# An attention block and two MLPs on one core: results of the second MLP turned by VectorE in 32 by 32 blocks and stored with short runs

## The chip, the cores and the metric

The kernel runs on one core of one Trainium2 chip. The metric is the device time of one execution in microseconds (us). The five engines are TensorE (PE, with its weight loads as PEld), VectorE (DVE), ScalarE (ACT), GpSimd (POOL) and SyncE (SP), which here issues nearly all transfers between the on-chip memory (SBUF) and the device's memory. The transfers of the core run on 16 transfer engines (DMA).

## What is computed

```python
# q, k, v: (8, 8, 576, 64) float32
q_s = softmax(q, axis=-1); k_s = softmax(k, axis=2)
x = q_s @ (k_s.T @ v)                       # per batch and head
x = x.transpose(0, 2, 1, 3).reshape(4608, 512)
h = x @ moe_w_in                            # (512, 2048)
x = (h * clip(h + 3, 0, 6) / 6) @ moe_w_out # (2048, 512)
h = x @ moe2_w_in
out = (h * sigmoid(h)) @ moe2_w_out         # (4608, 512) float32
```

The products are kept near float32 accuracy by splitting each operand into an upper and a lower part and adding three products (upper by upper, upper by lower, lower by upper).

## The kernel before

The 4608 rows are cut into nine blocks of 512. Attention and most of the first MLP run first (`first_block`, `middle`). From about 731 us on, `second_mlp` works in five passes (`PASSES`), each over two neighbouring blocks: four passes of the second MLP, on blocks 1 and 2, 3 and 4, 5 and 6, 7 and 8, and, after the first of them, one pass of the first MLP on blocks 7 and 8. Block 0 comes last, in a plain loop. The passes use seven products in place of eight (Strassen's scheme), on sums of quarters of the weights that were stored to memory (`ws`) before.

A pass has 56 inner steps (`inner`, L1330, products with the first weight matrix, tile `pb`) and 56 outer steps (`outer`, L1500, products with the second one), six matmuls of 128x512 each, one step after the other on TensorE. The weights come through a ring of six places (`ring`): a place holds two parts, each of which serves one step, and `fetch` (L1177, 512 KB) fills it again once its last step is done, for the step that comes six places later. Meanwhile `x_ahead` prepares the operands of the next pass: loads (L1460, tile `xst`), splits on ScalarE and VectorE (tile `gsp`), stores to `xd` (L1470, L1471) and later a load back.

The order is written out by hand: `when(t, fn)` files a piece of work under a time counted in steps, the list is sorted by this time, and every engine gets its instructions in that order. SP works through its list in order too: a transfer that waits for data holds up those behind it. Successive transfers of SP use eight completion counters (DMAHW0 to DMAHW7) in turn, and each waits until the one eight before it has landed.

At the end of a pass of the second MLP the result lies in eight tiles of 128x512 (`fixed`), transposed: rows are columns of the result, columns are the 512 rows of a block. `turn` brings it into place. It runs eight times per pass, every five steps from about four steps after the pass's end on, that is, between the inner steps of the next pass (`bank` gives it one of eight PSUM banks in turn). For the last pass of all, it runs in the loop over block 0, once in each of its first eight steps, with a bank of `a_pool`. One `turn` makes four transposes of 128x128 on TensorE against the identity `ident` (L1545, four matmuls with an identity operand), copies the 128x512 result from PSUM to SBUF on ScalarE (L1549, tile `o2`, which the trace and the order call `o`) and stores it with one transfer of 256 KB (L1551), in which each of the 128 partitions writes one run of 2 KB.

The operation that the change uses stands already in the stage before: `q_blocks` (L479) turns a 128x512 tile on VectorE in blocks of 32 by 32, `q_store` writes it, and `q_load` (L489) reads it back with four transfers of 32 partitions and runs of 128 B.

Of the kernel before, what the change touches and what calls it, by code (L numbers as in the profile page):

```python
# [18 lines left out]
P = 128  # L19
BLK = 512  # L20
# [8 lines left out]
def efficient_attention_then_two_mlps(  # L29
# [11 lines left out]
    nc = tc.nc  # L41
# [4 lines left out]
    NC = DM // P  # L46
    NF = DFF // P
    NB = NT // BLK
    NCH = BLK // P
# [6 lines left out]
    PASSES = ((1, 1), (0, NCL)) + tuple((1, j) for j in range(3, NB, 2))  # L56
# [14 lines left out]
    ident = const.tile([P, P], F32, name="ident")  # L71
# [4 lines left out]
    small = const.tile([P, 8], F32, name="small")  # L76
# [637 lines left out]
    for i, u in enumerate(range(2, NP)):  # L714
        o = i * (KB + VB + QB)
# [115 lines left out]
    for j in range(1, NB):  # L831
        for pr in range(NP):
            n = (j - 2) * NP + pr
# [326 lines left out]
    def when(t, fn):  # L1160
        ev.append((t, len(ev), fn))
# [7 lines left out]
    def bank():  # L1169
        pool, tag = BANKS[taken[0] % 8]  # L1170
        taken[0] += 1
        return pool.tile([P, 512], F32, tag=tag, name="pb")
# [126 lines left out]
    def second_mlp(last):  # L1299
        fixed = []  # L1300
# [12 lines left out]
        def small(name, tag="t2k"):  # L1313
            return tmp.tile([P, BLK], F32, tag=tag, bufs=1 if tag == "r" else 5, name=name)
# [4 lines left out]
        d = {}  # L1319
# [214 lines left out]
            for k, (name, m) in enumerate((name, m) for name in names for m in range(2)):  # L1534
                when(t + k, lambda m=m, name=name: do(m, name))

        def turn(j, k, bank=bank):

            h, i = (1, k) if k < NCH else (0, k - NCH)
            at = bank()  # L1540
            for a in range(2):
                for m in range(2):
                    x = fixed[4 * m + ((3, 1), (0, 2))[a][h]]
                    c = 2 * a + m
                    nc.tensor.transpose(  # L1545
                        at[:, c * P : (c + 1) * P], x[:, i * P : (i + 1) * P], ident
                    )
            o = small("o2")
            nc.scalar.copy(o, at)  # L1549
            rows = out[(j + h) * BLK : (j + h + 1) * BLK, :].rearrange("(p i) d -> i p d", i=NCH)  # L1550
            nc.sync.dma_start(rows[i], o)  # L1551

        T = 0.0
        uses = {}
        BB = len(PASSES)
        for b, (ph, j) in enumerate(PASSES):
# [35 lines left out]
            if b + 1 < BB:  # L1592
# [6 lines left out]
                            lambda n=n, low=low: x_fetch(n, low),  # L1599
                        )  # L1600
                for k in range(2 * NCH if ph else 0):
                    when(T + 3.95 + 5.0 * k, lambda j=j, k=k: turn(j, k))
            else:
                def begin_last():
                    op.pop("spare")
# [20 lines left out]
        for f in range(NF):  # L1626
            s = (1, 0, f)
            mm1(s)
            if f < 2 * NCH:
                turn(PASSES[-1][1], f, a_pool)  # L1630
            gate(s, lambda: None)
            if prev is not None:
                mm2(prev)
            if f % 2 == 0:
                load_split(f + 1, 1)
            prev = s
# [57 lines left out]
```

## Time and profile before

| | us |
|---|---|
| median of three runs | 1607.06 (1603.67 to 1607.39) |
| profiled execution | 1605.05 |
| its span, first to last instruction | 1603.3 |
| TensorE busy | 1573.6 |
| VectorE busy | 1130.5 |
| ScalarE busy | 790.1 |
| GpSimd busy | 447.6 |

The span is a little shorter than the time of the execution. A line of the profile names a group of instructions by its line in the kernel, its engine and its operation, and gives what it writes and reads (`out<-in`). Matmuls overlap, so that their durations cannot be added up; the distance between starts tells their cost. The share of the DMA engines is the mean over all 16.

The results are turned in four stretches: from 890 to 946 us (blocks 1 and 2), from 1199 to 1256 us (3 and 4), from 1354 to 1412 us (5 and 6), and from 1510 to 1552 us (7 and 8, in the loop over block 0). They are called the first to the fourth stretch below.

### The profile page before, as it was taken

The page shows a single profiled execution, that of the slowest core. Times are in us where ns is not written, and L with a number is a line of the kernel's source. Part 1 is how long each engine was busy: PE and PEld are TensorE (multiplying, and loading weights), DVE is VectorE, ACT ScalarE, POOL GpSimd, SP SyncE. Part 2 cuts the span into 40 slices and gives each one's busy share as a digit, 9 for nine tenths or more (in the row PEclk, how much of TensorE's full clock was granted, in tenths as well). Part 3 has the DMA queues.
Part 4 walks back from the last instruction along what each step waited for, and adds up shares of the span by engine and source line. Part 5 has one row for each costly group of instructions (what it writes and reads, how often), then busy time and mean ns, then how long its engine had stood idle before and what let it go on. Part 6 is the DMA issues. An engine that isn't in the chain of part 4 may idle for free.

```text
span 1603.3 us, 23117 instructions
## 1 busy us (share of the span) xinstructions
PE 1573.6 (98%) x7516; PEld 1288.0 (80%) x7516; DVE 1130.5 (71%) x1882; ACT 790.1 (49%) x1422; POOL 447.6 (28%) x417
## 2 busy tenths in 40 slices
PE   5999999999999999999999999999999999999998
PEld 3777888887878888888888888888888888888887
DVE  8989567777777787676877667667757775567522
ACT  5777345555554555454454445444534553445322
POOL 2002233334233344542410451045005500330000
PEclk9999999999999999999999999999999999999999
DMA  9913976777767776858987898898979886669730
GB/s 269 333 30 113 322 220 208 206 227 220 239 203 220 223 233 200 249 171 295 366 295 286 297 356 301 315 315 307 331 256 329 323 329 236 215 229 356 247 125 27
DMA packets 352426, 401.61 MB, mean 250 GB/s; under 512 B 120497, under 2 KB 233137, under 8 KB 352305
## 3 DMA queue, kind: packets, MB, share of 16 engines
q1 hardware_dynamic: 350256, 399.05, 74.6%
q8 instruction: 60, 0.98, 0.2%
q10 hardware_dynamic: 2048, 1.08, 0.2%
q14 instruction: 62, 0.50, 0.1%
HBM read 276.56 MB, written 123.47 MB: 250 GB/s over the span
## 4 chain that ended last, share of the span: by engine, by line
PE 93%; DMA 3%; SPq 2%; DVE 1%; ACT 1%; issue 0%; POOL 0%; ACTq 0%; DVEq 0%; POOLq 0%
PE pb L1500 24%; PE pb L1330 24%; PE h L562 20%; PE y L634 18%; PE y L636 3%; PE pa L516 2%; PE pa L398 1%; DMA wi_early<-in_moe_w_in_dram 1%; PE pb L1545 1%; DMA wo_early<-in_moe_w_out_dram 1%; SPq L100 0%; SPq L106 0%; DMA zd<-qz 0%; DMA ws<-fa 0%; DMA qraw<-in_q_dram 0%
## 5 line engine op out<-in xcount | busy, mean ns | idle before, releaser
L1330 PE MATMUL pb<-xo,ring 128*128 128x512 f32 x1680 | 390.6, 391 | 0.4 <-ACT s L1370 0.4
L562 PE MATMUL h<-x,wi 128*128 128x512 f32 x1536 | 381.5, 395 | 3.7 <-ACT g L610 1.9
L1500 PE MATMUL pb<-gsp,ring 128*128 128x512 f32 x1680 | 382.4, 389 | 0.0
L1500 PEld LDWEIGHTS pb<-gsp,ring 128*128 128x128 f32 x1680 | 315.3, 188 | 65.5
L1330 PEld LDWEIGHTS pb<-xo,ring 128*128 128x128 f32 x1680 | 313.3, 188 | 66.3 <-ACT s L1370 1.5
L562 PEld LDWEIGHTS h<-x,wi 128*128 128x128 f32 x1536 | 284.6, 189 | 67.1 <-ACT g L610 3.8
L634 PE MATMUL y<-g,wo 128*128 128x512 f32 x1344 | 326.3, 392 | 1.2 <-DVE o L653 1.2
L634 PEld LDWEIGHTS y<-g,wo 128*128 128x128 f32 x1344 | 252.4, 189 | 54.7 <-DVE o L653 1.6
L1317 DVE TENSOR_TENSOR gsp<-g,gsp 128x512 fp32r<-128x512 f32 x240 | 171.5, 722 | 72.1 <-ACT gsp L1435 69.2
L1435 ACT CAST gsp<-g 128x512 fp32r<-128x512 f32 x240 | 144.3, 622 | 139.4 <-DVE gsp L1317 70.1
L575 ACT ACTIVATE r<-h 128x512 f32<-128x512 f32 x112 | 66.9, 597 | 177.0 <-PE h L562 173.7
L1317 POOL TENSOR_TENSOR s<-U,s 128x512 f32<-128x512 f32 x32 | 44.7, 1395 | 383.7 <-DVE U L1317 368.7
L599 DVE SCALAR_TENSOR_TENSOR h<-r,h 128x512 f32<-128x512 f32 x112 | 77.5, 692 | 77.6 <-ACT r L575 77.1
L1317 DVE TENSOR_TENSOR g<-r,pb 128x512 f32<-128x512 f32 x96 | 65.6, 683 | 47.6 <-ACT r L1344 47.5
L1344 ACT ACTIVATE r<-pb 128x512 f32<-128x512 f32 x96 | 57.1, 595 | 70.9 <-DVE pb L1317 60.1
L437 POOL TENSOR_TENSOR qe<-qraw,qm 128x512 f32<-128x512 f32 x34 | 40.2, 1181 | 172.1 <-DVE qz L479 130.3
L590 ACT CAST g<-h 128x512 fp32r<-128x512 f32 x112 | 65.6, 585 | 45.5 <-DVE h L599 37.6
L1317 POOL TENSOR_TENSOR g<-g 128x512 f32<-128x512 f32 x40 | 54.9, 1372 | 91.9 <-DVE g L1317 79.9
L593 DVE TENSOR_TENSOR g<-h,g 128x512 fp32r<-128x512 f32 x96 | 66.0, 687 | 20.3 <-ACT g L590 18.9
L463 POOL TENSOR_TENSOR qe<-qe,qs 128x512 f32<-128x512 f32 x36 | 39.5, 1097 | 122.0 <-DVE qs L459 96.7
L195 POOL TENSOR_TENSOR fa<-fa 128x256 f32<-128x256 f32 x64 | 49.6, 775 | 55.3 <-DVE sp L227 50.2
L1317 DVE TENSOR_TENSOR U<-pb,s 128x512 f32<-128x512 f32 x80 | 54.7, 684 | 13.6 <-PE pb L1330 8.4
(166 smaller groups left out, 1830.4 us busy)
## 6 DMA issues: line engine op xcount, KB each, us to landing
ring<-ws SPq DMA_DIRECT2D x280, 512.0 KB, 5.1
ws<-sp SPq DMA_DIRECT2D x256, 128.0 KB, 2.2
xd<-gsp SPq DMA_DIRECT2D x112, 256.0 KB, 5.5
xo<-xd SPq DMA_DIRECT2D x56, 512.0 KB, 6.0
wi_early<-in_moe_w_in_dram SPq DMA_DIRECT2D x16, 512.0 KB, 9.0
wo_early<-in_moe_w_out_dram SPq DMA_DIRECT2D x16, 512.0 KB, 8.9
wi_raw<-in_moe_w_in_dram SPq DMA_DIRECT2D x16, 512.0 KB, 4.8
ws<-w_sum SPq DMA_DIRECT2D x64, 128.0 KB, 2.0
```

Of the source, the lines that this page charges most:

```text
L195: lambda to=to, x=x, y=y, op=op: nc.gpsimd.tensor_tensor(out=at[to], in0=at[x], in1=at[y], op=op)
L562: nc.tensor.matmul(h, w[:, a, c, :], x[:, e, c, :], start=(c == 0 and n == 0), stop=(c == NC - 1 and n == 2),)
L575: nc.scalar.activation(self.r, self.h, AF.Relu, bias=3.0)
L590: nc.scalar.copy(self.g[:, 0], self.r)
L593: nc.vector.tensor_tensor(out=self.g[:, 1], in0=self.r, in1=f32(self.g[:, 0]), op=ALU.subtract)
L599: nc.vector.scalar_tensor_tensor(out=self.h, in0=self.r, scalar=6.0, in1=self.h, op0=ALU.min, op1=ALU.mult)
L634: nc.tensor.matmul(y[c], w[:, a, cs], g[:, e, :], start=st, stop=sp)
L1317: (eng or nc.vector).tensor_tensor(out=out, in0=a, in1=b, op=how)
L1330: nc.tensor.matmul(to, ws_[:, a], e[:, c], start=p in ("P1", "P6", "P5") and c == 0 and m == 0, stop=c == 1 and m == 2, skip_group_check=True,
L1344: nc.scalar.activation(r, d[b, n, key], AF.Sigmoid)
L1435: nc.scalar.copy(t[0], source(p, i))
L1500: nc.tensor.matmul(d[b, p][m], w[:, a, m * P : (m + 1) * P], t[e], start=new and i == 0 and k == 0, stop=i == NPR - 1 and k == 2, skip_gro ...
```

## The change

`turn` gives way to `turn_blocks`, which is called at the same times, eight times per pass. Each call takes one of the eight result tiles (128 columns of the result by 512 rows), transposes it on VectorE in 64 blocks of 32 by 32, and stores it with four transfers of 32 partitions, 64 KB each; a partition then writes 16 runs of 32 numbers (128 B). The first call of a pass writes into a new tile `o2`, each later one into the tile whose contents were transposed by the call before (`gone`). TensorE, ScalarE and PSUM have no part in it any more.

```diff
-        def turn(j, k, bank=bank):
-
-            h, i = (1, k) if k < NCH else (0, k - NCH)
-            at = bank()
-            for a in range(2):
-                for m in range(2):
-                    x = fixed[4 * m + ((3, 1), (0, 2))[a][h]]
-                    c = 2 * a + m
-                    nc.tensor.transpose(
-                        at[:, c * P : (c + 1) * P], x[:, i * P : (i + 1) * P], ident
-                    )
-            o = small("o2")
-            nc.scalar.copy(o, at)
-            rows = out[(j + h) * BLK : (j + h + 1) * BLK, :].rearrange("(p i) d -> i p d", i=NCH)
-            nc.sync.dma_start(rows[i], o)
+        gone = []
+
+        def turn_blocks(j, k):
+            h, n = (1, k) if k < NC else (0, k - NC)
+            a, m = divmod(n, 2)
+            x = fixed[4 * m + ((3, 1), (0, 2))[a][h]]
+            o = gone.pop() if k else small("o2")
+            gone.append(x)
+            nc.vector.transpose(o, x)
+            rows = out[(j + h) * BLK : (j + h + 1) * BLK, n * P : (n + 1) * P]
+            for i in range(4):
+                e = slice(i * 32, i * 32 + 32)
+                nc.sync.dma_start(
+                    rows[:, e].rearrange("(b r i) c -> r i b c", b=4, i=NCH),
+                    o[e].rearrange("r (i b c) -> r i b c", i=NCH, b=4),
+                )
...
-                    when(T + 3.95 + 5.0 * k, lambda j=j, k=k: turn(j, k))
+                    when(T + 3.95 + 5.0 * k, lambda j=j, k=k: turn_blocks(j, k))
...
-                turn(PASSES[-1][1], f, a_pool)
+                turn_blocks(PASSES[-1][1], f)
```

SP at the start of the first stretch, before (`o` is the turned tile, `xst` and `xd` belong to the operands of the next pass; the brackets name what an instruction waits for):

```order
L1460 DMA xst<-yd 128x512 [waits DMAHW3_49]
L1551 DMA out_dram<-o_9030 128x512 [waits DMAHW4_49,Activation_49]
L1177 DMA ring<-ws 128x2x512 [waits DMAHW5_49,PE_49]
L1177 DMA ring<-ws 128x2x512 [waits DMAHW6_49,PE_49]
L1470 DMA xd<-gsp 128x512 [waits DMAHW7_49,Activation_49]
L1471 DMA xd<-gsp 128x512 [waits DMAHW0_49,DVE_49]
L1177 DMA ring<-ws 128x2x512 [waits DMAHW1_49,PE_49]
L1551 DMA out_dram<-o_9098 128x512 [waits DMAHW2_49,Activation_49]
```

The same place on SP after the change:

```order
L1460 DMA xst<-yd 128x512 [waits DMAHW3_49]
L1551 DMA out_dram<-o_9025 128x4x32 [waits DMAHW4_49,DVE_49]
L1551 DMA out_dram<-o_9025 128x4x32 [waits DMAHW5_49]
L1551 DMA out_dram<-o_9025 128x4x32 [waits DMAHW6_49]
L1551 DMA out_dram<-o_9025 128x4x32 [waits DMAHW7_49]
L1177 DMA ring<-ws 128x2x512 [waits DMAHW0_49,PE_49]
L1177 DMA ring<-ws 128x2x512 [waits DMAHW1_49,PE_49]
L1470 DMA xd<-gsp 128x512 [waits DMAHW2_49,Activation_49]
L1471 DMA xd<-gsp 128x512 [waits DMAHW3_49,DVE_49]
L1177 DMA ring<-ws 128x2x512 [waits DMAHW4_49,PE_49]
L1551 DMA out_dram<-vbuf 128x4x32 [waits DMAHW5_49,DVE_49]
```

Between one turn and the next SP has the same three refills of the ring and the same two stores, behind four short-run stores in place of one plain store, and the turn's first store waits for VectorE instead of ScalarE.

VectorE at the second turn of the first stretch, before (`U`, `s` and `pb` are sums of the inner products, `g` the gated ones, `gsp` a lower half):

```order
L1353 SCALAR_TENSOR_TENSOR g_7711<-r_9063,pb 128x512
L1317 TENSOR_TENSOR gsp<-xst,gsp 128x512
L1317 TENSOR_TENSOR U_9091<-pb,s_9073 128x512
L1317 TENSOR_TENSOR pb<-s_8998,pb 128x512
L1353 SCALAR_TENSOR_TENSOR g_7755<-r_9109,pb 128x512
```

The same place on VectorE after the change:

```order
L1353 SCALAR_TENSOR_TENSOR g_7711<-r_9061,pb 128x512
L1317 TENSOR_TENSOR gsp<-xst,gsp 128x512
L1317 TENSOR_TENSOR U_9089<-pb,s_9071 128x512
L1547 STREAM_TRANSPOSE vbuf<-fin 128x512
L1317 TENSOR_TENSOR pb<-s_8998,pb 128x512
L1353 SCALAR_TENSOR_TENSOR g_7755<-r_9104,pb 128x512
```

One transpose has been put in, between the sum `U` and the next sum; the instructions around it keep their order.

## Rows read from the trace of the kernel before

**Rows 1.** The page: span, and busy time of the engines.

```profile
span 1603.3 us, 23117 instructions
...
PE 1573.6 (98%) x7516; PEld 1288.0 (80%) x7516; DVE 1130.5 (71%) x1882; ACT 790.1 (49%) x1422; POOL 447.6 (28%) x417
```

**Rows 2.** Waits of TensorE from 888 us to the end (all of them).

```profile
engine line waited for: us in total, times, longest us
PE pb L1330 <- ACT s L1370: 0.4, 1, 0.4
```

**Rows 3.** Transposes of line L1545: duration min/median/max in ns, first and last start.

```profile
L1545 PE MATMUL pb<-ident,fin x48: 271/272/273, 891.1 to 1408.2; 128*128 128x128 f32 x48
```

**Rows 4.** Timeline of TensorE in the first stretch: start, us, what.

```profile
898.30 0.27 PE L1545 MATMUL pb<-ident,vbuf 128*128 128x128 f32 x1
...
898.66 7.10 PE L1330 MATMUL pb<-xo,ring 128*128 128x512 f32 x30
905.60 0.27 PE L1545 MATMUL pb<-ident,vbuf 128*128 128x128 f32 x1
```

**Rows 5.** Timeline of TensorE in the loop over block 0.

```profile
1519.53 0.27 PE L1545 MATMUL pa<-ident,vbuf 128*128 128x128 f32 x1
...
1525.46 0.27 PE L1545 MATMUL pa<-ident,vbuf 128*128 128x128 f32 x1
...
1552.40 2.88 PE L562 MATMUL h<-x,wi 128*128 128x512 f32 x12
1555.12 2.88 PE L636 MATMUL y<-wo,g 128*128 128x512 f32 x12
1557.84 2.88 PE L562 MATMUL h<-x,wi 128*128 128x512 f32 x12
```

**Rows 6.** Busy time of the engines in the four stretches, with DMA share and GB/s.

```profile
core 0: us, PE busy (x) PEld busy (x) DVE busy (x) ACT busy (x) POOL busy (x), PEclk, DMA share, GB/s
890.00:946.00 56.00, 56.00 (x262) 45.91 (x261) 38.35 (x54) 27.80 (x52) 30.62 (x23) 1.00 0.96 342
1199.00:1256.00 57.00, 57.00 (x268) 47.07 (x267) 40.33 (x55) 28.01 (x52) 31.22 (x23) 1.00 0.97 344
1354.00:1412.00 58.00, 58.00 (x272) 47.87 (x271) 29.69 (x44) 22.15 (x40) 20.30 (x16) 1.00 0.67 214
1510.00:1552.00 42.00, 42.00 (x202) 34.64 (x201) 10.36 (x15) 13.38 (x24) 0.00 (x0) 1.00 0.31 109
```

**Rows 7.** Line L479, the transposes on VectorE in the stage before.

```profile
L479 DVE STREAM_TRANSPOSE qz<-qe x27: 696/703/712, 167.7 to 688.1; 128x512 f32<-128x512 f32 x27
```

**Rows 8.** Line L1549, ScalarE's copies of turned results (24 of 32).

```profile
L1549 ACT COPY o<-pb x24: 575/587/606, 891.6 to 1408.5; 128x512 f32<-128x512 f32 x24
```

**Rows 9.** Transfers from 627.2 to 627.8 us: packets, and the queue's share.

```profile
DMA packets 464, 0.06 MB, mean 96 GB/s; under 512 B 464, under 2 KB 464, under 8 KB 464
...
q1 hardware_dynamic: 464, 0.06, 61.2%
```

**Rows 10.** Transfers of the first stretch: GB/s in 40 slices, and packets.

```profile
GB/s 356 313 402 389 354 214 297 158 161 375 402 408 402 358 337 176 399 401 408 345 217 222 377 395 255 222 348 399 399 322 377 405 389 401 326 357 394 410 407 398
DMA packets 10199, 19.15 MB, mean 342 GB/s; under 512 B 871, under 2 KB 871, under 8 KB 10195
```

**Rows 11.** Ring refills in the first, then in the third stretch: issue to landing.

```profile
DMA to landing us min/median/max: 4.0/5.9/6.9
...
DMA to landing us min/median/max: 3.4/4.1/4.8
```

**Rows 12.** SP: four short-run loads, a plain store's issue (ns), refills' waits.

```profile
625.75 2.61 SPq L489 DMA_DIRECT2D qt<-zd x4
...
L1551 SPq DMA_DIRECT2D out_dram<-o x32: 337/342/784, 892.3 to 1550.4; - x32
...
SPq L1177 <- PE pb L1330: 115.9, 87, 3.6
```

## What I expect, and why

> **What bounds the kernel now.** I read the page first. TensorE is busy for 1573.6 of 1603.3 us, VectorE for 71% [rows 1], so time goes only where TensorE's own work goes, unless something new makes it wait. The reader is to see next that in the part that the change touches (from 888 us to the end: the second MLP's passes and the last block) TensorE waits once, for 0.4 us [rows 2]. So no wait can be won here; what can be won is TensorE's time for the transposes, and what can be lost is a wait that does not exist yet. The third reading is what the transposes cost, from the distance between starts on TensorE [rows 4, 5], because the duration of one (272 ns, [rows 3]) overlaps the next. The fourth is how full the transfer engines are in the four stretches where the results are turned: shares of 0.96, 0.97, 0.67 and 0.31 [rows 6]. TensorE is granted full clock in all four.
>
> **What the change removes from TensorE.** 32 turns of four transposes. In a pass, 30 matmuls and one turn take 905.60 - 898.30 = 7.30 us [rows 4]. In the last block, 24 matmuls without a turn take 1557.84 - 1552.40 = 5.44 us, 227 ns each; with a turn they take 1525.46 - 1519.53 = 5.93 us [rows 5]. Thirty matmuls alone are then 30 x 0.2267 = 6.80 us, and a turn costs 7.30 - 6.80 = 0.50 us in a pass and 0.49 us in the last block. There are 24 turns of the first kind and 8 of the second: 12.0 + 3.9 = 15.9 us, all on the path, since TensorE does not wait there. What is late next after TensorE? Nothing is, by [rows 2]; the stretches only become shorter by 8 x 0.49 = 3.9 us each. The clock gives nothing: it is at 1.00 already.
>
> **What leaves ScalarE.** 32 copies of 0.587 us [rows 8], 18.8 us. ScalarE is busy for 27.8 of 56 us in the fullest stretch [rows 6] and TensorE does not wait for it: worth nothing. The eight PSUM banks that the turns of a pass took are a whole round of eight, so the products after them get the same banks as before; between turns a bank now comes round later. Nothing waited for one: nothing again. Seven of the eight output tiles per pass vanish too, since a turned block goes into the tile that was turned before it.
>
> **What VectorE gets.** 32 transposes of 128x512. The trace has this very operation and shape, 27 times, between 696 and 712 ns [rows 7], so the price is 0.703 us, 5.6 us per stretch. VectorE is busy for 38.4 of 56, 40.3 of 57, 29.7 of 58 and 10.4 of 42 us [rows 6]; with 5.6 more and 3.9 us less time it would be at 84%, 86%, 65% and 42%. The cover is its own idle time, and the products that it hands back lie in a round of eight banks. The input of each transpose was finished a pass earlier, so it adds no wait of its own; behind it on VectorE stand the gate's multiplications and sums. If that cover were gone, the cost would be 0.70 us a turn.
>
> **What SP gets.** Each turn now issues four transfers where it issued one. Four of this shape (32 partitions, runs of 128 B, 64 KB) took SP 2.61 us in the stage before [rows 12], against some 0.34 us for one plain store: 2.3 us more a turn. Behind them on SP stand the refills of the weight ring, then stores and loads of the next pass's operands. SP has room: it waits 87 times, up to 3.6 us, for TensorE to release a ring place [rows 12], that is, it is early. A wait for VectorE's transpose takes the place of a wait for ScalarE's copy, at about the same place in the program. I cost the issuing at nothing on the path.
>
> **What the transfer engines get.** This is the term that decides. Per turn 128 runs of 2 KB become 2048 runs of 128 B, in the same 256 KB. The trace before has no store to memory with runs that short. The nearest row is the reverse way, loads from memory with runs of 128 B and the same shape, 64 KB at a time: 464 packets kept 16 engines busy for 61.2% of 0.6 us [rows 9], so 0.612 x 0.6 x 16 / 464 = 12.7 ns a packet. As the upper bound stands the mean packet of the fullest stretch, nearly all of 2 KB: 0.96 x 56 x 16 / 10199 = 84 ns [rows 6, 10]. A lower one than 12.7 ns is not excluded by a row, but even a packet for nothing gives TensorE no more than the 15.9 us. I take 12.7 ns, as the row differs from the new store in direction alone.
>
> A turn then costs 2048 x 12.7 / 16 = 1.63 us of all engines. The old one cost its share of the bytes: 0.96 x 56 us for 19.15 MB, and 0.262 MB of it 0.74 us. That is 0.89 us more a turn, 7.1 us in a stretch of eight. In the first stretch the engines have between 56 x 0.04 = 2.2 us left (by the share) and 56 - 19.15 / 0.405 = 8.7 us (by the 405 GB/s that its best slices reach [rows 10]), and TensorE takes 3.9 us of time away. The engines end such a stretch 7.1 + 3.9 - (2.2 to 8.7) = 2.3 to 8.8 us behind. The second stretch is like the first. In the third, a third of 58 us is free and in the fourth two thirds of 42 us; there is no backlog.
>
> How late may a refill be? A ring place holds two parts and there are six places. The refill is issued when the place's last matmul is done, and is used after the other five places, ten steps of six matmuls: 10 x 6 x 0.2267 = 13.6 us. Refills land after 5.9 us in the first stretch, 6.9 us at most, and 4.8 us at most in the third [rows 11]. So 13.6 - 6.9 = 6.7 us of backlog costs nothing, and the stall is 0 to 2.1 us in each of two stretches. I take 0.5 us for each, 1 us in all; both ends are kept.
>
> **The sum.** Profiled execution 1605.05 us (span 1603.3): 1605.05 - 15.9 + 1.0 = 1590.2 us. The median of the three runs, 1607.06, lies 2.0 us above the profiled one, so I forecast 1592 us.
>
> **Rivals.** (a) *The short stores are dear, and the ring starves: slower than before.* Place: the first and second stretch, where the engines are full; price: the packet. At p ns a packet, a stretch falls 8 x (0.128p - 0.74) + 3.9 - (2.2 to 8.7) us behind, less 6.7 us of slack. The 15.9 us are gone when each stretch loses 7.9 us, which is at p between 18 and 25 ns. If a store of 128 B is twice the load, 25.4 ns, the two lose 9 to 15 us each, the third none (20.1 + 3.9 - 19.1 = 4.9 us behind, under its slack), and the time is 1607.1 - 15.9 + (17 to 30) = 1608 to 1621 us. At 84 ns it would be some 70 us each in two stretches, and 55 in each of the others, near 1840 us. For it speaks that no row shows such a store; against it, that the loads of the same shape did not hold up the stage before.
> The Trainium skill, "DMA: Bandwidth & Descriptors", section "Specifications", speaks for this rival: it asks for at least 512 B for line rate and says that below it the engine does a read-modify-write, which as an estimate is the doubled price of this rival; the rows here show only that a load of 128 B runs cost 12.7 ns, and no run so far shows the store.
> (b) *The freed time is not won where the transfers are the limit.* In the first two stretches the engines are at 0.96 and 0.97, and TensorE, faster by 0.5 us a turn, asks for the next weights earlier; SP's 2.3 us of issuing comes on top, and every transfer waits until the one eight before it has landed, so slow ones hold up refills. Then only the third and fourth stretch win, 16 x 0.49 = 7.9 us: 1607.1 - 7.9 = 1599 us. For it speaks the upper end of the backlog; against it, that refills with 6.9 us to land never stopped TensorE.
> (c) *VectorE becomes the one waited for.* If each transpose delayed a product that TensorE needs, 32 x 0.70 = 22.5 us come for 15.9 us: 1614 us. Against it stands VectorE's idle share, some 14% in the tightest stretch.
> (d) *The change does not take the transposes off TensorE*: excluded, the new order has none there.
>
> **How the numbers follow.** About 0.3% (4.8 us) is what a measurement of this kernel tells from no change: faster is under 1602.2, slower above 1611.9. Forecast 0.58 (all faster). Rival (b) 0.16, of it 0.10 faster and 0.06 the same. Rival (a) 0.22, of it 0.07 the same and 0.15 slower. Rival (c) 0.04, slower. So faster 0.68, same 0.13, slower 0.19. The range goes from 1587 (no stall at all, and the median on the profiled run's side) to 1612; some 0.02 lies below it and 0.17 above.
>
> **What would show each step.** Right: starts of TensorE 6.8 us apart where they were 7.3; no wait for a ring transfer; transposes on VectorE near 0.70 us; shares of the transfer engines near 1 in the first two stretches, refills landing in under 13 us there. Rival (a) or (b): TensorE waits for the ring between 888 and 960 us and again some 310 us later, but not in the last two stretches; packets of more than 18 ns. Rival (c): TensorE waits for VectorE's results. The forecast is wrong if a 128 B store costs much more than a load, or if issuing four transfers takes SP so long that refills come late.

## The result, and the profile of the changed kernel

| | before | after |
|---|---|---|
| median, us | 1607.09 (1603.67 to 1609.03, 6 runs) | 1616.47 (1614.87 to 1617.04, 6 runs) |
| profiled execution, us | 1605.05 | 1617.0 |
| its span, us | 1603.3 | 1615.3 |

The ratio is 1.0066, interval 1.0055 to 1.0077: the change makes the kernel slower by 9.4 us. The forecast was 1592 us, in a range up to 1612 us; the measured time lies above both. The profiled execution before lies 2 us under its median, so the two profiles differ by 12 us.

The page of the changed kernel, against [rows 1]. In the last line: busy time, mean ns of one, then idle time before the group and what ended most of it.

```profile
span 1615.3 us, 22931 instructions
...
PE 1567.9 (97%) x7388; PEld 1280.7 (79%) x7388; DVE 1143.3 (71%) x1914; ACT 773.1 (48%) x1390; POOL 447.6 (28%) x417
...
L1330 PE MATMUL pb<-xo,ring 128*128 128x512 f32 x1680 | 390.7, 393 | 19.3 <-DVE U L1317 12.8
```

TensorE has 128 instructions fewer, but it now stands idle before the inner steps. Its waits from 888 us to the end, all of them, where [rows 2] had one of 0.4 us (us in total, times, longest):

```profile
PE pb L1330 <- DVE U L1317: 12.8, 2, 6.4
PE pb L1330 <- ACT s L1370: 4.5, 1, 4.5
PE pb L1330 <- DMA ring<-ws: 1.0, 3, 0.5
```

These are 18.3 us. The timeline of TensorE (start, us, what, idle time before it and its releaser) places them: one stop in the first stretch, one behind it, one in the second stretch. The first line is from the kernel before, the start of the same steps.

```profile
885.57 5.61 PE L1330 MATMUL pb<-xo,ring 128*128 128x512 f32 x24
...
887.41 44.07 PE L1330 MATMUL pb<-xo,ring 128*128 128x512 f32 x192
937.89 26.86 PE L1330 MATMUL pb<-xo,ring 128*128 128x512 f32 x108 [6.41 <-DVE U L1317]
...
975.23 2.93 PE L1330 MATMUL pb<-xo,ring 128*128 128x512 f32 x6 [4.49 <-ACT s L1370]
...
1259.62 29.30 PE L1330 MATMUL pb<-xo,ring 128*128 128x512 f32 x120 [6.39 <-DVE U L1317]
```

The windows (columns as in [rows 6]) show a second loss: TensorE starts again after each long stop at half its clock.

```profile
936.00:937.00 1.00, 0.00 (x0) 0.00 (x0) 1.00 (x2) 0.00 (x0) 0.00 (x0) 0.50 0.87 248
938.00:942.00 4.00, 4.00 (x10) 3.13 (x11) 2.97 (x4) 2.59 (x5) 3.44 (x3) 0.50 1.06 390
943.00:960.00 17.00, 17.00 (x76) 14.08 (x76) 12.73 (x20) 7.43 (x14) 12.65 (x9) 1.00 0.95 284
...
1354.00:1412.00 58.00, 58.00 (x258) 48.04 (x257) 34.25 (x53) 18.50 (x33) 14.00 (x11) 1.00 0.70 211
1510.00:1552.00 42.00, 42.00 (x187) 34.80 (x186) 20.04 (x32) 12.42 (x21) 0.00 (x0) 1.00 0.75 219
```

The granted clock falls to 0.50 while TensorE stands still, and TensorE then works at 0.50 for 4.6, 4.7 and 3.6 us behind the three stops. Half of that is lost: 6.4 us. The balance of the two profiles: -15.9 us of transposes + 18.3 - 0.4 us of waits + 6.4 us of clock = +8.4 us. Another 1.8 us lie before anything that the change touches (887.41 against 885.57 us, above). Of the 12.0 us between the spans, 1.8 us are not placed. In the third and fourth stretch TensorE runs without a stop at full clock.

**What TensorE waited for.** ScalarE and VectorE just before the first stop ends:

```profile
935.30 0.62 ACT L1464 CAST gsp<-xst 128x512 fp32r<-128x512 f32 x1 [6.93 <-DMA xst<-yd]
...
935.95 0.69 DVE L1317 TENSOR_TENSOR gsp<-xst,gsp 128x512 fp32r<-128x512 f32 x1 [7.21 <-ACT gsp L1464]
936.56 0.70 DVE L1547 STREAM_TRANSPOSE vbuf<-fin 128x512 f32<-128x512 f32 x1
937.19 0.65 DVE L1317 TENSOR_TENSOR U<-pb,s 128x512 f32<-128x512 f32 x1
```

The sum U that frees TensorE's bank was not late by its own inputs. It stands on VectorE behind the split of the next pass's operands (`gsp`), which waited for ScalarE's half of that split, which waited for the loads of `xst`. SP issued these loads late. SP in the first stretch after the change (start, us that the issue took, what), each group of four being one turn's short stores:

```profile
900.87 2.73 SPq L1551 DMA_DIRECT2D out_dram<-vbuf  x4
903.70 2.56 SPq L1177 DMA_DIRECT2D ring<-ws  x1
...
909.25 3.56 SPq L1551 DMA_DIRECT2D out_dram<-fin  x4
...
924.95 4.48 SPq L1551 DMA_DIRECT2D out_dram<-fin  x4
929.53 1.38 SPq L1177 DMA_DIRECT2D ring<-ws  x1
931.01 1.83 SPq L1460 DMA_DIRECT2D xst<-yd  x4
```

The same loads in the kernel before, and who waited for them there from 888 to 960 us:

```profile
922.90 2.46 SPq L1460 DMA_DIRECT2D xst<-yd  x4
...
POOL xst L1317 <- DMA xst<-yd: 5.5, 1, 5.5
...
ACT gsp L1464 <- DMA xst<-yd: 1.9, 1, 1.9
```

They are issued 8.1 us later than before, of which 1.8 us lie before the stretch. Adding up SP's issues from 888 to 960 us gives 59.9 of 72 us, against 30.7 before, and 20 refills of the ring went out in that time instead of 25. Little of SP's time went on transfers that had yet to land: its waits for them add up to 1.8 us there, so the eight counters are not what holds it. It is the issuing of the four loads that is late and not their transfer; before, then after:

```profile
DMA to landing us min/median/max: 6.7/6.9/7.0
...
DMA to landing us min/median/max: 4.2/5.7/5.9
```

And before the change already, ScalarE and GpSimd waited for these loads: they had no slack.

The stop behind the first stretch (4.49 us, for `s`) has another late transfer at its root. ScalarE's copy of `s` stands behind a cast that waited for an earlier store of operands to land:

```profile
973.59 0.62 ACT L1435 CAST gsp<-g 128x512 fp32r<-128x512 f32 x1 [7.52 <-DMA xd<-gsp]
```

### The profile page after: what moved, and what is told of

It reads as the page before. It is cut to its first block, busy times and chain, and to the rows that moved or that the text cites. A ratio compares the mean times of both kernels' runs of the same rounds, so it can differ in the third digit from the quotient of the medians.

```text
span 1615.3 us, 22931 instructions
## 1 busy us (share of the span) xinstructions
PE 1567.9 (97%) x7388; PEld 1280.7 (79%) x7388; DVE 1143.3 (71%) x1914; ACT 773.1 (48%) x1390; POOL 447.6 (28%) x417
## 3 DMA queue, kind: packets, MB, share of 16 engines
q10 hardware_dynamic: 2048, 1.08, 0.2%
## 4 chain that ended last, share of the span: by engine, by line
PE 86%; DMA 5%; DVE 4%; ACT 2%; issue 1%; POOL 1%; SPq 1%; ACTq 0%; DVEq 0%; POOLq 0%
PE pb L1500 24%; PE h L562 21%; PE y L634 18%; PE pb L1330 17%; PE y L636 3%; PE pa L516 2%; DMA xd<-gsp 1%; PE pa L398 1%; DMA ring<-ws 1%; DMA xst<-yd 1%; DMA yd<-o 0%; DVE gsp L1317 0%; POOL s L1317 0%; DVE g L1317 0%; DMA xst<-xq 0%
## 5 line engine op out<-in xcount | busy, mean ns | idle before, releaser
L1330 PEld LDWEIGHTS pb<-xo,ring 128*128 128x128 f32 x1680 | 317.9, 190 | 90.0 <-DVE U L1317 13.8
L1317 DVE TENSOR_TENSOR gsp<-xst,gsp 128x512 fp32r<-128x512 f32 x56 | 51.7, 924 | 20.5 <-ACT gsp L1464 20.2
```

The lines of the kernel that those rows point to most:

```text
L1317: (eng or nc.vector).tensor_tensor(out=out, in0=a, in1=b, op=how)
L1330: nc.tensor.matmul(to, ws_[:, a], e[:, c], start=p in ("P1", "P6", "P5") and c == 0 and m == 0, stop=c == 1 and m == 2, skip_group_check=True,
```

## The experiments

The theory after the trace: SP is held while it gives out the short stores, and the operand loads behind them come late. The rivals: the short runs fill the transfer engines, and everything lands late; four transfers in place of one are the price; it is VectorE's transposes. Each kernel was timed beside the kernel before; the ratio is to that. Its interval reaches 0.001 to 0.002 to each side, 2 to 3 us, so a difference of 3 us between two of these kernels says little. Where a kernel leaves something out (the right placing of the results, or part of the weights), its expectation says so.

### Which part of the change costs the time

`one_plain`: VectorE's turn with one plain store.

```diff
-            for i in range(4):
...
+            nc.sync.dma_start(out[(j + h) * BLK + n * P : (j + h) * BLK + (n + 1) * P, :], o)
```

> VectorE's transposes as in the change, but one plain transfer of 256 KB per turn (128 partitions, runs of 2 KB, to a wrong place: the placing is left out), as many transfers as before the change. Theory 1 (SP is what is late): SP has the load that it had before, nothing is late, and the whole 15.9 us are won: 1591 us. Rival (VectorE's transposes cost TensorE something in the crowded stretches): 1596 us or more, with waits of TensorE for VectorE in the first two stretches.

Measured: 1592.24 us, 0.9909 (0.9889 to 0.9929). TensorE waits twice, 0.5 us in all. The gain was sized right, VectorE's transposes cost nothing that shows, and the loss lies in the stores.

`four_plain`: the same with four transfers of 32 partitions, runs of 2 KB.

```diff
+            flat = out[(j + h) * BLK + n * P : (j + h) * BLK + (n + 1) * P, :]
             for i in range(4):
...
+                nc.sync.dma_start(flat[e], o[e])
```

> VectorE's transposes as in the change, four transfers of 32 partitions and 64 KB per turn on SP as in the change, but each partition writes one run of 2 KB (to a wrong place in the output: the placing is left out). Theory 1 (SP: issuing four short-run transfers takes it so long that the next pass's operands are loaded late, ScalarE and VectorE wait for them and TensorE behind them): plain issues are short, 4 x 0.34 = 1.4 us a turn, SP keeps up, time near 1592 us. Rival (the number of transfers, not their runs, is too much for eight counters): still near 1610 us or more. Rival (VectorE's transposes hold TensorE up): still 1616 us.

Measured: 1598.92 us, 0.9949 (0.9931 to 0.9967). Four transfers cost 6.7 us more than one.

`one_short`: one transfer with all 2048 runs of 128 B.

```diff
-            for i in range(4):
...
+            wide = out[(j + h) * BLK : (j + h + 1) * BLK, n // 2 * 2 * P : (n // 2 + 1) * 2 * P]
+            wide = wide.rearrange("(p i) (b t c) -> p i b t c", i=NCH, b=4, t=2)
+            nc.sync.dma_start(
+                wide[:, :, :, n % 2], o.rearrange("p (i b c) -> p i b c", i=NCH, b=4)
+            )
```

> VectorE's transposes as in the change, and one transfer per turn with all 2048 runs of 128 B (columns are permuted: the right placing is left out). It has the runs of the change and the number of transfers of before. If the number of transfers on SP (four issues, four of the eight counters) is what makes SP late: 1591 to 1597 us. If SP's issuing time goes with the runs (0.64 us for 512 runs against 0.34 us for 32 or 128): one issue takes about 2 us or more, and the time lies near the change's, 1608 to 1618 us.

Measured: 1618.25 us, 1.0071 (1.0056 to 1.0086), as slow as the change with its four. Where the runs are short, the number of transfers no longer matters. SP in that kernel:

```profile
900.47 0.64 SPq L1551 DMA_DIRECT2D out_dram<-vbuf  x1
901.20 4.97 SPq L1177 DMA_DIRECT2D ring<-ws  x1
...
937.91 0.61 SPq L1551 DMA_DIRECT2D out_dram<-vbuf  x1
938.62 6.19 SPq L1177 DMA_DIRECT2D ring<-ws  x1
```

These are the clearest rows of the study. The short store itself is issued in 0.6 us, and the next transfer, an ordinary refill, then takes 5 to 6 us to issue (3.9 to 6.2 us over the first two stretches, 0.3 to 2.0 us in the other two). SP pays for the short runs with the instruction behind them.

`pe_short`: TensorE's turn of the kernel before, its result stored by four transfers of short runs.

```diff
-            nc.sync.dma_start(rows[i], o)
+            for q in range(4):
+                nc.sync.dma_start(
+                    rows[i].rearrange("p (b t c) -> p b t c", b=4, t=4)[:, :, q],
+                    o[:, q * P : (q + 1) * P].rearrange("p (b c) -> p b c", b=4),
+                )
```

> The kernel before the change, turned by TensorE as there, but each turn's result is stored with four transfers of 64 KB with runs of 128 B instead of one with runs of 2 KB (columns of the output are permuted: the right placing is left out). Only the change's store is in it, without its transposes. Theory 1: the loss comes from the store alone, some 25 us (what the change lost against 1591 us), less what TensorE's slower pace gives SP back (8 x 0.5 us in each of two stretches): 1620 to 1632 us. Rival (the store is harmless by itself and the loss comes from VectorE's transposes among its other work): 1607 us.

Measured: 1628.07 us, 1.0131 (1.0116 to 1.0147). The short stores alone cost the kernel before 21 us, with no transpose on VectorE.

### Whether it takes crowded transfer engines

`late_only`: the change in the third and fourth stretch, TensorE's turn in the first two.

```diff
-   when(T + 3.95 + 5.0 * k, lambda j=j, k=k: turn_blocks(j, k))
+   when(T + 3.95 + 5.0 * k, lambda j=j, k=k: (turn_blocks if j == 5 else turn)(j, k))
```

> The change only in the third and fourth stretch (blocks 5 to 8); the first two passes' results are turned by TensorE as before. There SP has little else to issue and the engines are at 0.67 and 0.31. Theory 1 and the transfer-engine rival alike: 16 turns x 0.49 = 7.9 us are won and nothing lost, 1599 us. If VectorE's transposes or the end of the kernel were the cause of the loss, it stays at 1607 us or above.

Measured: 1597.71 us, 0.9942 (0.9927 to 0.9957). The half of the change with room on the transfer engines gains 9.1 us, and this kernel beats both.

`mixed`: as `late_only`, but the first four turns of each crowded pass by the change too.

```diff
+   when(T + 3.95 + 5.0 * k, lambda j=j, k=k: (turn_blocks if j == 5 or k < NC else turn)(j, k))
```

> The change in the third and fourth stretch, and in the first two only for the first four turns of each pass; the other four are made by TensorE as before. The engines' extra time in the two crowded stretches is halved, to 3.6 us each. If nothing were late at that load: 1597.7 - 8 x 0.5 = 1594 us. If the first two stretches have no room at all (the engines at 0.96 and the loads of the next operands without slack): each loses about what it wins, 1596 to 1602 us.

Measured: 1609.98 us, 1.0013 (1.0003 to 1.0022). That is above both of its expected ranges. Four short turns in a crowded stretch are enough: TensorE waits 11.5 us in two waits for U, because the operand loads stand behind these four (issued at 927.59 us).

`half_ring`: the change, with the refills of the inner steps cut to half their bytes in the two crowded passes.

```diff
+        w = 1 if o == 0 and b in (1, 3) else 2
...
-            f32(ring[k % len(ring)]),
...
+            f32(ring[k % len(ring)])[:, 0:w],
+            ws[PASSES[b][0], o, 2 * m : 2 * m + w].rearrange("s p d -> p s d"),
```

> The change, but in the inner steps of the two passes in which the first and second stretch lie, each refill of the weight ring brings one part of 256 KB instead of two (the second part's weights are left out, so products there use old ones). The short-run stores are as in the change; only the other load of the transfer engines is lighter, by some 5 MB in a stretch of 19 MB. If the transfer engines' time is what runs out (0.96 of it was used before, the short runs ask for 0.89 us more a turn): they now have room, and the whole gain comes out, 1590 to 1594 us. If SP is held up by the short runs as such, whatever else the engines carry: still 1608 us or more.

Measured: 1595.54 us, 0.9921 (0.9903 to 0.9939). The transfer engines' share from 900 to 930 us falls to 0.85 (0.96 in the change), and the same short stores come to 3.3 us over `one_plain`. SP in that kernel (line numbers are one higher), to set beside the rows of after at 924.95 us:

```profile
921.95 2.62 SPq L1552 DMA_DIRECT2D out_dram<-fin  x4
924.67 0.56 SPq L1178 DMA_DIRECT2D ring<-ws  x1
925.33 1.81 SPq L1461 DMA_DIRECT2D xst<-yd  x4
```

Four short stores take 2.6 to 3.3 us to issue here (2.6 us in [rows 12], 2.6 to 2.7 us in the fourth stretch of the change) and hold little up behind them. So the whole loss needs short runs and crowded engines together; crowded engines without short runs cost 6 to 12 us (`four_plain` above, and the plain loads below).

### Moving the work out of the way

`x_later`: the splits of the second half's operands six steps later in the two crowded passes, their loads where they were.

```diff
+   when(t - (10.0 if c and b in (2, 4) else 4.0) + 0.3 * m, lambda n=n: load(n))
+   x_ahead(b + 1, 1, t0 + (34.0 if b in (1, 3) else 28.0), 3.0)
```

> The change, but in the first two stretches the second half of the next pass's operands is split six steps (some 8 us) later, while its loads keep their place; so a load that comes up to 8 us late holds nobody up. Theory 1 in this form (the late loads of these operands are what stops ScalarE, then VectorE, then TensorE for 6.4 us in each of the two stretches): these two stops go, together with the slow matmuls after them; time 1598 to 1608 us. Rival (SP and the transfers are behind altogether, and the next late transfer stops TensorE instead, a refill or a store that releases a tile): 1612 us or more.

Measured: 1616.76 us, 1.0065 (1.005 to 1.008), no gain. The waits of TensorE in it:

```profile
PE pb L1330 <- DMA ring<-ws: 10.4, 6, 4.1
PE pb L1330 <- ACT s L1370: 4.9, 1, 4.9
```

The wait for U is nearly gone (1.2 us) and the next late transfer takes its place, the refill of the ring. The operand loads are only the first to be late; SP is behind with everything.

`spread`: turns every seven steps in place of five.

```diff
-   when(T + 3.95 + 5.0 * k, lambda j=j, k=k: turn_blocks(j, k))
+   when(T + 3.95 + 7.0 * k, lambda j=j, k=k: turn_blocks(j, k))
```

> The change with its turns every seven steps (9.5 us) instead of every five (6.8 us). Theory 1: SP has 9.5 us for what took it some 8 us per turn in the crowded stretches, so it keeps up; TensorE's long waits in the first two stretches shrink to a third or go; 1593 to 1603 us. Rival (one particular late transfer, not SP's rate): 1612 us or more, as before.

Measured: 1611.22 us, 1.0028 (1.0017 to 1.004): 5 us back, between the two expected times. Each group of four still takes 3.3 to 4.5 us in the first stretch.

`act_queue` and `pool_queue`: the four stores issued from ScalarE, or from GpSimd.

```diff
-                nc.sync.dma_start(
+                nc.scalar.dma_start(
...
+                nc.gpsimd.dma_start(
```

> The change, but its four short-run transfers per turn are issued from ScalarE instead of SP. Theory 1 (SP's issuing time): SP is as free as before, the loads of the next operands go out in time; the time falls below 1605 us unless ScalarE, which then spends some 2.6 us more per turn and waits for VectorE's transpose and for counters in its own row, becomes the late one. Rival (the 16 transfer engines cannot carry the short runs in time): nothing changes, 1612 to 1620 us, and the loads land late although they are issued in time.

> The change, with its four short-run stores issued from GpSimd in place of SP. Nothing else is moved, so the transfer engines have the same runs to carry. If what costs time is that SP is held while the runs wait, SP is free again: its loads of the operands are issued near 922 us, TensorE does not wait for them, and the time is 1594 to 1604 us, less what GpSimd loses by issuing (it was busy for 31 of 56 us in that stretch). If the transfer engines themselves are behind with the short runs, the loads are issued in time and land late, and TensorE waits as in the change: 1612 us or more.

Measured: 1653.26 us, 1.0291 (1.0274 to 1.0308), and 1799.29 us, 1.1198 (1.1181 to 1.1215). Neither tells what it was meant to, since the new issuer is held in place of SP, with its own work behind (ScalarE for 2.6 to 4.3 us per group of four in the first stretch). First the kernel with ScalarE (the two largest of TensorE's waits), then the one with GpSimd (TensorE's only wait from 888 us on, and GpSimd's timeline):

```profile
PE pb L1330 <- ACT s L1370: 25.2, 10, 5.2
PE y L636 <- ACT g L590: 11.4, 5, 9.3
```

```profile
PE pb L1330 <- ACT s L1364: 160.0, 18, 13.4
...
939.68 0.74 POOL L1551 DMA_DIRECT2D out_dram<-kbuf  x1
942.22 0.74 POOL L1551 DMA_DIRECT2D out_dram<-kbuf  x1 [1.80 <-issue]
```

GpSimd needs 2.5 us for one such store.

### The time on the transfer engines, or the number of runs

First the price of a run, which decided rival (a). In the fourth stretch of the change the queue carried nothing but short stores from 1532.5 to 1535.4 us:

```profile
DMA packets 2373, 0.30 MB, mean 102 GB/s; under 512 B 2373, under 2 KB 2373, under 8 KB 2373
...
q1 hardware_dynamic: 2373, 0.30, 58.7%
```

0.587 x 2.9 x 16 / 2373 = 11.5 ns a run, a little under the 12.7 ns of the load in [rows 9]. The doubled price, which I had estimated from the read-modify-write that the Trainium skill names for transfers under 512 B ("DMA: Bandwidth & Descriptors", section "Specifications"), is not what this row shows. A turn's 2048 runs take 1.47 us (at 12.7 ns 1.63 us) of all engines, a plain store 0.74 us.

`double_plain`, `match_plain`, `triple_plain`: plain stores, with a second one of 256 KB to memory that nothing reads; then a third of 64 KB, or of 256 KB. By bytes that is 1.48, 1.66 and 2.22 us of all engines a turn.

```diff
+            nc.sync.dma_start(xq[h, n], o)
...
+            nc.sync.dma_start(zd[k, 0:32], o[0:32])
...
+            nc.sync.dma_start(zd[k], o)
```

> VectorE's transposes with one plain store per turn (to a wrong place, the placing is left out), and a second plain store of the same tile to a scratch place: no short run anywhere, one issue of 0.34 us more on SP and 256 KB more for the engines, 0.74 us a turn against the 0.89 us that the short runs add. If the transfer engines' time is what runs out: most of the loss comes back, 1606 to 1614 us, at 0.74/0.89 of the change's loss. If short runs as such hold SP up: 1592 to 1596 us, like the one plain store.

> VectorE turns; one plain store of 256 KB and, as pure load, a second one of 256 KB and a third of 64 KB (runs of 2 KB) into memory that nothing reads: 2.25 times the bytes of a turn. By 0.74 us of all transfer engines for 256 KB a turn takes 1.66 us of them, as much as the 2048 short runs of the change at 12.7 ns each (1.63 us). The result rows land in other places than the reference wants. If the loss goes with the time on the transfer engines, it is as slow as the change: 1612 to 1620 us, with TensorE waiting some 18 us. If it needs the short runs themselves, it lies on the line through 1592 us (one plain store) and 1598 us (two): 1599 to 1603 us, and SP's issues stay under 1 us.

> As match_plain with the third store of 256 KB too: three times the bytes of a turn, 2.22 us of all transfer engines, 0.6 us more than the short runs of the change take. If the loss goes with the time on the transfer engines: beyond the change, 1622 us or more. If it needs the short runs themselves: 1602 to 1610 us.

Measured: 1598.31 us, 0.9938 (0.9923 to 0.9953); 1602.44 us, 0.9974 (0.9963 to 0.9985); 1604.62 us, 0.9988 (0.9977 to 0.9998). The same time on the engines as the short runs take (1.47 to 1.63 us a turn), in runs of 2 KB, costs 6 to 10 us over `one_plain`; half as much again costs 12 us; the change costs 24 us. The first stretch from 900 to 930 us, `double_plain` and then `triple_plain`:

```profile
900.00:930.00 30.00, 30.00 (x134) 24.63 (x133) 24.10 (x35) 12.88 (x24) 17.06 (x13) 1.00 1.03 373
...
900.00:930.00 30.00, 28.21 (x125) 23.04 (x123) 21.06 (x31) 11.85 (x23) 13.39 (x10) 1.00 1.04 378
```

The engines are no less full there than under the change (share 0.96, 290 GB/s in the same window; a share above 1 can only mean that packets' times overlap, so all of these are full), and yet TensorE loses less. Their time explains some 10 of the 24 us.

The path is the same and the cause on SP is not. In `match_plain` too the operand loads are late, ScalarE and GpSimd wait for them (4.0 and 7.6 us), and TensorE waits 7.1 us in two waits for U. But there SP's issues from 888 to 960 us add up to 37.2 us, none above 1.2 us, and it waits some 15 us for transfers to land, against 1.8 us in the change.

`one_512` and `one_256`: one transfer a turn, in 512 runs of 512 B, or in 1024 runs of 256 B.

```diff
+            rows = out[(j + h) * BLK : (j + h + 1) * BLK, n * P : (n + 1) * P]
+            nc.sync.dma_start(
+                rows.rearrange("(p i) c -> p i c", i=NCH), o.rearrange("p (i c) -> p i c", i=NCH)
+            )
...
+            wide = wide.rearrange("(p i) (b t c) -> p i b t c", i=NCH, b=2, t=2)
+            nc.sync.dma_start(
+                wide[:, :, :, n % 2], o.rearrange("p (i b c) -> p i b c", i=NCH, b=2)
+            )
```

> VectorE turns as in the change, and one transfer stores the turned tile with 512 runs of 512 B: each of the 128 partitions writes four of them. The values land in other rows of the output than the reference wants. Plain stores (128 runs of 2 KB) gave 1592 us, one transfer with 2048 runs of 128 B gave 1618 us. If the price goes with the number of runs in a straight line, 512 of them cost (512 - 128) / (2048 - 128) of those 26 us, 5.2 us: 1597.5 us, and SP's issue behind such a store takes some 1.5 to 2 us in the first stretch. If SP is held up only once the runs are more than what can be queued, or if only runs under some length are dear, nothing is lost: 1592 to 1594 us, and the issue behind the store takes under 1 us. If the strided placement itself, rather than the number of runs, is dear: 1610 us or more.

> VectorE turns as in the change, and one transfer stores the turned tile with 1024 runs of 256 B (eight a partition; the values land in other places than the reference wants). 512 runs of 512 B gave 1592.7 us, no more than plain stores, and 2048 runs of 128 B in one transfer 1618 us. If the price starts where the runs that wait fill what SP can queue, 1024 of them lie between: SP's issue behind the store takes 1.5 to 3 us in the first stretch, and the time is 1596 to 1608 us. If only the time of the transfer engines counts, at 12.7 ns a run the 1024 take 0.81 us of all engines where the plain store took 0.74 us, 0.6 us more in a whole stretch: 1592 to 1594 us, and SP's issues stay under 1 us. If every run under 512 B is dear: near 1618 us.

Measured: 1592.7 us, 0.9911 (0.9895 to 0.9928), and 1594.01 us, 0.9922 (0.9905 to 0.9938). One transfer with 128, 512, 1024 and 2048 runs gives 1592.2, 1592.7, 1594.0 and 1618.3 us: no straight line, but a step behind 1024. SP in `one_256`, at the place where `one_short` shows 5 to 6 us:

```profile
918.31 0.62 SPq L1550 DMA_DIRECT2D out_dram<-fin  x1
919.02 0.74 SPq L1177 DMA_DIRECT2D ring<-ws  x1
919.86 2.08 SPq L1460 DMA_DIRECT2D xst<-yd  x4
```

In these kernels number and length of the runs change together; the next experiment keeps both.

### The same runs, given out apart

`apart`: the change with all its runs and its four transfers a turn, but each of the four is issued 1.25 steps after the last.

```diff
-            for i in range(4):
...
+        def place_block(j, k, i):
+            rows, o = placed[j, k]
+            e = slice(i * 32, i * 32 + 32)
...
+                    for i in range(4):
+                        when(T + 3.96 + 5.0 * k + 1.25 * i, lambda j=j, k=k, i=i: place_block(j, k, i))
```

> The change with the same four short-run stores of a turn, which are now issued one at a time, 1.25 steps (1.7 us) apart, in place of one behind the other; the turns themselves stay five steps apart, and in the last block nothing differs. Runs, bytes, transfers and the work of every engine are those of the change. If SP is held because 2048 short runs are given out at once, and 1024 at a time cost nothing: each issue takes some 0.6 to 0.9 us, the loads of the operands are issued near 925 us, and the time is 1594 to 1603 us. If what counts is how many short runs there are in the whole stretch, SP is held as long, in smaller pieces: 1612 to 1618 us.

Measured: 1599.76 us, 0.9958 (0.9941 to 0.9975). With the same runs, bytes and transfers 16.7 of the 24 us are back. SP and TensorE's waits in it:

```profile
921.36 0.60 SPq L1556 DMA_DIRECT2D out_dram<-fin  x1
922.05 0.60 SPq L1177 DMA_DIRECT2D ring<-ws  x1
922.75 1.88 SPq L1460 DMA_DIRECT2D xst<-yd  x4
...
PE pb L1330 <- ACT s L1370: 3.3, 1, 3.3
PE pb L1330 <- DVE U L1317: 2.3, 2, 1.2
```

The operand loads go out at 922.75 us, as in the kernel before. SP is still busy: its issues from 888 to 960 us add up to 56.1 us against 59.9, but 26 refills and 28 operand stores have gone out in that time, where the change got out 20 and 22. One thing besides the pauses differs: three of a turn's four stores now stand behind the operand loads. Of the 8.3 us by which the loads go out earlier than in the change, some 4 us are this order and 1.6 us lie before the stretch; the rest is that SP was less held before it. The 7.5 us that `apart` stands above `one_plain` are as much as twice the plain bytes (6.1 us) or four transfers (6.7 us) cost.

`apart_early`: as `apart`, with the operand loads two steps earlier in the two crowded stretches.

```diff
+   when(t - (6.0 if c and b in (2, 4) else 4.0) + 0.3 * m, lambda n=n: load(n))
```

> As apart, and the loads of the operands for the second half are issued two steps (2.7 us) earlier in the first two stretches, so that on SP they stand ahead of two or three of the short stores and one refill that stood before them. In apart TensorE still waited 5.6 us in these stretches, of it 2.3 us in two waits for U, behind the splits that wait for these loads. If these are what is left of the lateness: 1596 to 1598 us, and no wait for U. If the loads only push refills and stores back by as much: 1599 to 1602 us, the waits being elsewhere.

Measured: 1602.29 us, 0.9966 (0.9952 to 0.998). The waits for U are gone, others (7.1 us, mostly for `s` of ScalarE) have taken their place: no gain.

## Why the prediction was wrong

**TensorE's 15.9 us: right.** In the last block of the changed kernel, 24 matmuls with a turn start 5.44 us apart, as those without one did in [rows 5]:

```profile
1547.96 2.88 PE L562 MATMUL h<-x,wi 128*128 128x512 f32 x12
...
1553.40 2.88 PE L562 MATMUL h<-x,wi 128*128 128x512 f32 x12
```

`one_plain` came to 1592.2 us, 14.6 us under the kernel before beside it.

**VectorE, ScalarE, PSUM: right.** The transposes took 694 to 707 ns, and rival (c) fell with `one_plain`.

**The price of a run: right** (11.5 ns in a row without other traffic; among full engines it was not measured by itself). With it rival (a)'s doubled price falls. Its place was the right one, and its time, 1608 to 1621 us, holds the result by luck, since the loss came another way.

**"What the transfer engines get": too small.** The forecast put 1.0 us for the backlog, 0 to 2.1 us in each of two stretches. As much time on the engines in plain runs costs some 10 us (`match_plain`, which also has two more issues a turn), because the backlog meets the operand loads and not the ring.

**"What SP gets": the step that failed.** It counted 2.3 us more a turn and then "cost the issuing at nothing on the path", because SP waits 87 times for ring places [rows 12]. The 87 waits are those of the whole program; from 888 to 960 us there were 10. Even so, at that price the first stretch would have had room: 30.7 us of issues and eight times 2.3 us make 49 of 72 us. The price itself was wrong. 2.61 us for four short transfers was read in a stage with room on the engines; with full engines SP took 2.7 to 4.5 us for the four and up to 2.6 us for the transfer behind them. So the operand loads went out late, and TensorE lost 17.9 us in waits and 6.4 us by the clock. The step should have asked what an issue costs in the stretch where it will stand. `one_short`, `half_ring` and `apart` show this hold.

**"How late may a refill be?": asked of the wrong load, and too generous.** TensorE waited only 1.0 us for the ring in the change, but it was already stopped for the operand loads; in `x_later`, without that stop, it waited 10.4 us for refills. So the 6.7 us of slack did not cover what SP made late. The operand loads of the next pass, on the same queue, had no slack at all: ScalarE waited 1.9 us and GpSimd 5.5 us for them before the change, and VectorE's U stands behind what waits for them. [rows 2] showed TensorE's waits alone; those of the engines one step ahead of it would have shown where lateness passes straight through.

**Rival (b)** named SP's issuing and slow transfers holding up what is behind them, and the two stretches, but held that TensorE would only not win there. It lost 17.9 us in waits there and 6.4 us by the clock, a term that no part of the sum had.

**What the 24 us over plain stores are made of.** Shown: 16.7 us come back when the same 2048 runs are given out apart (`apart`). That kernel also changes the order on SP, and the two were not separated; `apart_early` speaks against the order as the cause, since loads that go out earlier still gained nothing there. The rest, 7.5 us, is of the size of what the added engine time or the added transfers cost by themselves; how it divides between them was not separated either. Open stays what inside SP's issue waits while the engines are full, since no row of the trace shows it; that the runs fill what can be queued fits the step between 1024 runs of 256 B and 2048 of 128 B in one transfer, and is argued only.

## What to carry to other kernels

A store in short runs has two prices: its time on the transfer engines, and the time that the issuing queue is held, which falls on the instruction behind it and grows when the engines are full. Read the price of an issue from the stretch where it will stand, and look for slack in every load behind it on that queue, through the engines that feed TensorE and not in TensorE's waits alone. If short runs are needed, give them out in small transfers with other work between them, or only where the engines have room: both kept about half of the 14.6 us or more here (1599.8 and 1597.7 us).

## What the runs showed of the hardware that I had not expected

- With full engines, the issue that follows a transfer of 2048 runs of 128 B took 3.9 to 6.2 us (`one_short`), behind one of 1024 runs of 256 B at most 1.7 us (`one_256`), and the short transfer's own issue 0.6 to 1.0 us in both.
- Runs of 256 B cost the kernel 1.8 us over runs of 2 KB by the medians, runs of 512 B 0.5 us; neither is clear of the noise.
- A stop of TensorE costs more than its length. The granted clock fell to 0.50 (1.2 in place of 2.4 GHz) during the stops of 6.41, 4.49 and 6.39 us, and TensorE then worked at it for 4.6, 4.7 and 3.6 us before 1.00 came back: 6.4 us lost beside 18.3 us of waits.
